# The MLP's second stage by seven half products, and pooling by adding DMAs, in a fused attention and mixer kernel

## The chip, the cores and the metric

The kernel runs on one core of one Trainium2 chip. The core has TensorE (PE, matrix products; PEld is its weight load), VectorE (DVE), ScalarE (ACT) and GpSimd (POOL). SyncE (SP), ACT and POOL issue DMAs. Each engine works through its own queue in order and waits on semaphores for the others. The metric is device time in microseconds (us), from the start to the end of one execution. A TensorE matmul takes a weight tile of 128 x 128 and streams up to 512 columns past it into one bank of PSUM, the accumulation memory; DVE or ACT drain the bank.

## What is computed

```
for each of 8 batches, 8 heads, 576 rows, head size 64:
    k_p, v_p = means of k, v over groups of 8 rows        # 72 rows
    attn     = softmax(q @ k_p.T / 8)
    x[:, head] = attn @ v_p                               # x: 576 x 512 a batch
u   = x + (relu(x.T @ w_tok1) @ w_tok2).T                 # mixes the 576 rows, hidden 256
out = u + relu(u @ w_ch1) @ w_ch2                         # mixes the 512 columns, hidden 1536
```

Inputs and output are float32; the products run on bfloat16 copies.

## The kernel before

**Units.** The last line above, the MLP, is most of the products. It is cut into nine units. Unit n below 8 has 512 rows of batch n, unit 8 has the 64 rows left over from each of the eight batches (`uT_tails`, `u_tails`). `unit_steps` (L439) is a unit. Its first stage makes twelve tiles of relu(u @ w_ch1), 128 hidden values by 512 rows, each by four matmuls of 512 columns (L451) and a relu on ACT into GT (L455). A half tile is two of these matmuls. The second stage makes four blocks of 128 rows by 512 columns, each by twelve matmuls with a piece of GT as weights and w_ch2 streaming (L474). DVE drains a block, adding u (L479), and SP stores it in two halves (L482). In unit 8 the last block is made in two halves of 256 columns (L463).

**What runs between.** `unit_steps` yields after every second matmul, 48 times a unit. At each yield `unit` (L515) runs the steps that a plan names for that place: FIRST, SECOND and THIRD for units 0 to 2, LATER for the rest (L489 to L501). The order on every engine's queue is exactly the order in which these steps are recorded. A step without a mark is for the next batch, `>` for the one after that, `<` for the unit's own. The steps:

- `lk3 lv3 lq3`: load k, v or q of the batch three ahead, by a DMA issued on POOL that also converts to bfloat16.
- `K0 K1 V0 V1`: pool half of the heads on POOL (`pool8`, L143): three additions, L146, L147 and L150 (k) or L152 (v). `k1`, `v1`: the same on DVE.
- `kpT`: turn the pooled k on PE (L195), copied by DVE (L197). `Q0 Q1`: turn q on DVE (L244).
- `s0` to `s3`: scores, eight small matmuls (L255) and two exponentials on ACT (L261).
- `av0` to `av4`: attention times v, eight small matmuls (L293), a reciprocal and a scaling on DVE (L305, L311), which give x.
- `at0 at1`: the row-mixing hidden layer (L339), relu on ACT for the first half and on DVE for the second.
- `u0` to `u4`: its second layer (L354) and the addition of x on DVE (L355). `u4` is the leftover rows, once for two batches.
- `t0` to `t4`: turn u on PE (L364) with a copy on DVE (L365). From batch 4 on instead: `M0 M2 M4 M` write u to memory and read it back in pieces on SP, and `T0` to `T4` turn the pieces on DVE (L387, L393). The first stage of the next unit needs these.

Before unit 0 a HEAD of steps makes batch 0. PSUM has eight banks: three for single tiles (`ps_one`), four as two pairs for scores and av (`ps_two`), one for turned tiles (`ps_tr`).

Of the kernel before, what the change touches and what calls it, by code (L numbers as in the profile page):

```python
# [13 lines left out]
PE = mybir.EngineType.PE  # L14
POOLE = mybir.EngineType.Pool
DVE = mybir.EngineType.DVE
ACT = mybir.EngineType.Activation
SYNC = mybir.EngineType.SP


@with_exitstack
def kernel(
# [30 lines left out]
    singles = ctx.enter_context(tc.tile_pool(name="singles", bufs=1))  # L53
    raw = ctx.enter_context(tc.tile_pool(name="raw", bufs=2))
# [34 lines left out]

    def load_kv(b, src, key):  # L90
        t = loaded[b, key] = raw.tile([SP, H, POOL, D], BF16, name=key + "r")
        if b == 0:
            for h0, h1, j0, j1 in ((0, HP, 0, BP), (0, H, BP, SP), (HP, H, 0, BP)):
                kv(t, src, b, h0, h1, j0, j1)
        else:
            kv(t, src, b, 0, H)
# [59 lines left out]
    def batch_steps(b):  # L156
# [29 lines left out]
        def pool(eng, t, g):  # L186
            def go():
                hs = slice(g * HP, (g + 1) * HP)
                pool8(eng, loaded[b, t], hs, st["kp"][:, g] if t == "k" else st["vp"][:, hs, 0:D], t == "k")
            return go  # L190

        def kpT():
            ps = ps_tr.tile([P, 4, SP], BF16, name="pt")
            for i in range(4):
                nc.tensor.transpose(out=ps[:, i, :], in_=st["kp"][:, i // 2, i % 2].rearrange("j l d -> j (l d)"),  # L195
                                    identity=ident[0:SP, 0:SP])
            nc.vector.tensor_copy(out=st["kD"].rearrange("p g e j -> p (g e j)"), in_=ps.rearrange("p i j -> p (i j)"))  # L197
# [82 lines left out]
        def av(c):  # L280
            def go():
# [4 lines left out]
                den = outp.tile([P, 2, 4], FP32, name="den")  # L286
# [19 lines left out]
                if first and c == 1:  # L306
                    for h in range(H):
                        nc.scalar.activation(out=dst[:, h * D:(h + 1) * D], in_=view[:, h // 4, h % 4, 0:D],
                                             func=AF.Copy, scale=den[:, h // 4, h % 4:h % 4 + 1])
                else:  # L310
                    nc.vector.tensor_tensor(out=dst.rearrange("p (a h d) -> p a h d", a=2, d=D),  # L311
                                            in0=view[:, :, :, 0:D],
                                            in1=den[rows, :, :, None].broadcast_to([n, 2, 4, D]), op=ALU.mult)
# [14 lines left out]
        def relu(m, ps):  # L328
            if m == 0:
# [28 lines left out]
        def uT(c):  # L358
            def go():
                src = st["u"][:, c, :] if c < 4 else u_tails[:, b // 2, :]  # L360
                dst, o = (late("uT"), c * P) if c < 4 else (uT_tails, b // 2 * P)
                ps = ps_tr.tile([P, 4, P], BF16, name="pt")
# [54 lines left out]
        for g in range(2):  # L417
            name[f"vpool{g}"] = ppool(g)
# [6 lines left out]
        for i in range(4):  # L425
            name[f"Q{i}"], name[f"s{i}"] = (lambda: None) if i % 2 else qD(i // 2), score4(i // 2, i % 2)
        for c in range(5):
            name[f"av{c}"], name[f"u{c}"], name[f"t{c}"] = av(c), u(c), uT(c)
            name[f"at_{c}"], name[f"T{c}"] = at_tile(c), blocks(c)
# [9 lines left out]
    def unit_steps(n, st):  # L439

        GT = gtp.tile([P, NM, 4 * P], BF16, name="GT")
        uT = uT_tails if n == B else st["uT"]
        if n < B and "paired" in st:
            pairs = uT.rearrange("f k n -> f (k n)").rearrange("f (k n e) -> f k n e", k=2, e=2)
            blocks = [pairs[:, kk // 2, :, kk % 2] for kk in range(4)]
        else:
            blocks = [uT[:, kk, :] for kk in range(4)]
        for m in range(NM):
            ps = ps_one.tile([P, 512], FP32, name="p1")
            for kk in range(4):  # L450
                nc.tensor.matmul(out=ps, lhsT=w_ch1[:, kk, m * P:(m + 1) * P], rhs=blocks[kk],  # L451
                                 start=(kk == 0), stop=(kk == 3))
                if kk == 1:
                    yield
            nc.scalar.activation(out=GT[:, m, :], in_=ps, func=AF.Relu)  # L455
            yield
        for c in range(4):
            if n == B and c == 3:
                for a in range(2):
                    cols = slice(a * 256, (a + 1) * 256)  # L460
                    ps = ps_one.tile([P, 512], FP32, name="p1")
                    for m in range(NM):
                        nc.tensor.matmul(out=ps[:, 0:256], lhsT=GT[:, m, c * P:(c + 1) * P], rhs=w_ch2[:, m, cols],  # L463
                                         start=(m == 0), stop=(m == NM - 1))
                    o_sb = outp.tile([P, DM], FP32, name="o")[:, 0:256]
                    nc.vector.tensor_tensor(out=o_sb, in0=ps[:, 0:256], in1=(u_tails if n == B else st["u"])[:, c, cols], op=ALU.add)
                    for half in range(2):
                        (nc.scalar if half else nc.sync).dma_start(
                            out=out[2 * c + half].rearrange("(p r) n -> p r n", r=BR)[:, 8, cols],
                            in_=o_sb[half * BP:(half + 1) * BP, :])  # L470
                continue
# [6 lines left out]
            o_sb = outp.tile([P, DM], FP32, name="o")  # L478
            nc.vector.tensor_tensor(out=o_sb, in0=ps, in1=(u_tails if n == B else st["u"])[:, c, :], op=ALU.add)  # L479
            for half in range(2):  # L480
                b, r = (2 * c + half, 8) if n == B else (n, 2 * c + half)
                nc.sync.dma_start(out=out[b].rearrange("(p r) n -> p r n", r=BR)[:, r, :],  # L482
                                  in_=o_sb[half * BP:(half + 1) * BP, :])
            yield


    HEAD = """c0 c1 d8 q0 d1 q1 d5 kp0 kp1 kt0 d2 o0 e0 kt1 kp2 kp3 o1 e1 kt2 kt3 q2 q3 d2 o2 e2 vpool0 o3 d1 vpool1 e3 d2
              av1 av0 av2 d2 av3 at_0 at_2 av4 at_1 at_3 d2 at_4 X0 X1 X2 A0 A1 A2 X3 A3 d3"""
    FIRST = {0: "<u0 K0 lv2 V0", 1: "<u1", 2: "<u2", 3: "<u3 k1", 7: "Q0 Q1 Q2", 9: "Q3", 14: "kpT v1",  # L489
             16: "s0", 18: "s1", 20: "s2 lk3 lq3 lv3", 22: "s3", 24: "av0", 26: "av1", 28: "av2", 30: "av3", 32: "av4",  # L490
             34: "at0 >K0 >K1", 35: "at1 >V0", 37: "u0", 38: "u1", 39: "u2", 40: "t0", 41: "u3", 42: "t1 u4", 44: "t2", 45: "t3",
             47: "t4"}
    SECOND = {0: "kpT Q0 Q1 >K0 >K1 lk3", 1: "Q2 Q3 v1 lq3 lv3 >V0 >V1", 4: "s0", 6: "s1", 9: "s2", 12: "s3", 14: "av0", 16: "av1",
              18: "av2", 20: "av3", 22: "av4", 24: "at0", 25: "at1", 27: "u0", 28: "u1", 29: "u2 t0", 31: "u3 t1", 33: "t2 >Q0",
              35: "t3 >Q1", 37: ">kpT >Q2 >Q3", 39: ">s0", 42: ">s1", 45: ">s2", 47: ">s3"}
    THIRD = {0: ">K0 >K1 >V0 >V1 lk3 lq3 lv3", 1: "av0", 3: "av1", 5: "av2", 7: "av3", 9: "av4", 11: "at0 >Q0", 12: "at1",
             14: "u0", 15: "u1", 17: "u2 t0", 18: "u3", 19: "t1 u4", 21: "t2 >Q1", 23: "t3", 25: "t4 >kpT", 26: ">Q2 >Q3",
             27: ">s0", 29: ">s1", 32: ">s2", 35: ">s3", 38: ">av0", 40: ">av1", 42: ">av2", 44: ">av3", 46: ">av4"}
    LATER = {0: ">K0 >K1 >V0 >V1 lk3 lq3 lv3 at0", 1: "at1", 3: "u4 M4", 4: "u0", 6: "u1 M0", 7: "u2", 9: "u3 M2 M",
             11: ">Q0", 12: ">Q1", 14: ">Q2", 16: ">Q3", 18: ">kpT", 22: ">s0", 24: "T0", 26: ">s1 T1", 28: "T2",  # L500
             30: ">s2 T3", 32: "T4", 34: ">s3", 37: ">av0", 39: ">av1", 41: ">av2", 43: ">av3", 45: ">av4"}  # L501
    warm = singles.tile([P, 512], BF16)

    def head(s):
        if s[0] == "d":
            ps = ps_tr.tile([P, 512], FP32, name="pt")
# [8 lines left out]
    def unit(n, at):  # L515
        if n + 2 < B:
            batches[n + 2][0]()
        for i, _ in enumerate(unit_steps(n, batches[n][2] if n < B else None)):
            for s in at.get(i, "").split():
                if s[0] == "l":  # L520
                    load(s[1], n + int(s[2]))
                    continue
# [5 lines left out]
    with tc.manual_schedule(engines={PE, POOLE, DVE, ACT, SYNC}):  # L528
# [59 lines left out]
```

## Time and profile before

| | us |
|---|---|
| time, median of 3 runs | 285.08 (284.79 to 285.76) |
| the profiled execution | 285.26 |
| its span, first to last instruction | 283.5 |
| start of unit 0's first matmul | 24.95 |
| start of unit 7's first stage | 237.71 |
| end of the last matmul | 279.71 |

Parts of the profile that are read below: the page's busy times; stretches of the span with each engine's busy time; the chain that ended last, in order of time; groups of instructions by line and shape (instructions' total and mean time, then the idle time before them and what ended it); the timeline; and DMA issues with size and median time from issue to landing. L numbers are lines of the kernel.

### The profile page before, as it was taken

Reading aid. Unit: us, or ns where it says so; the run is one execution under the profiler, and the core shown is the slowest. Engines: PE = TensorE matmul, PEld = TensorE weight load, DVE = VectorE, ACT = ScalarE, POOL = GpSimd, SP = SyncE. Lnnn points to the kernel's source line nnn. Section 1 sums busy time; section 2 is a strip of 40 time slices with the busy share of each in tenths; the row PEclk is TensorE's granted clock in tenths of the full one; section 3 lists DMA queues with packets and bytes.
Section 4 is the critical chain, followed back from the end, with each engine's and each line's share of the span. In section 5 each row is a group of like instructions: output and inputs, shape, how many; then the busy total and the mean of one; then the engine's idle time right before and its main releaser. Section 6 shows DMA issues by size and latency. Waiting matters only on the chain.

```text
span 283.5 us, 4515 instructions
## 1 busy us (share of the span) xinstructions
PE 274.8 (97%) x1816; PEld 130.3 (46%) x1816; DVE 138.2 (49%) x265; ACT 110.3 (39%) x193; POOL 140.1 (49%) x124
## 2 busy tenths in 40 slices
PE   8999899999999999999999999999999999999994
PEld 3755335444553544354445443544354444444443
DVE  5466977777583756175247434833383141011012
ACT  2543481029404642604751366046603512612600
POOL 8584894999999939974993796000000000000000
PEclk9999999999999999999999999999999999999999
DMA  7999999960893187159649955325132445015014
GB/s 148 194 202 207 204 205 200 234 135 2 123 166 74 39 118 132 43 96 202 143 90 151 222 139 81 82 58 129 39 76 56 126 78 112 3 37 111 2 39 110
DMA packets 36837, 32.68 MB, mean 115 GB/s; under 512 B 14288, under 2 KB 30288, under 8 KB 36816
## 3 DMA queue, kind: packets, MB, share of 16 engines
q0 software_dynamic: 18672, 17.64, 39.2%
q1 hardware_dynamic: 17984, 14.62, 21.9%
q8 instruction: 14, 0.23, 0.3%
q10 hardware_dynamic: 160, 0.13, 0.2%
q14 instruction: 7, 0.06, 0.1%
HBM read 38.21 MB, written 11.80 MB: 176 GB/s over the span
## 4 chain that ended last, share of the span: by engine, by line
PE 91%; DVE 5%; ACT 2%; issue 1%
PE p L451 31%; PE p L474 31%; PE p L354 6%; PE p L339 5%; PE p L255 4%; PE p L293 3%; PE pt L508 3%; ACT ex L261 2%; PE pt L364 1%; DVE t L146 1%; PE p L463 1%; PE p L273 1%; PE p L322 1%; DVE qD L244 1%; PE p L411 1%; PE p L226 1%
## 5 line engine op out<-in xcount | busy, mean ns | idle before, releaser
L474 PE MATMUL p<-w_ch,GT 128*128 128x512 bf16 x420 | 102.3, 379 | 0.0
L451 PE MATMUL p<-uT,w_ch 128*128 128x512 bf16 x384 | 96.6, 383 | 0.0
L455 ACT ACTIVATE GT<-p 128x512 bf16<-128x512 f32 x108 | 64.3, 596 | 82.4 <-PE p L451 82.4
L451 PEld LDWEIGHTS <-w_ch 128*128 128x128 bf16 x432 | 39.8, 97 | 48.9 <-issue 4.1
L474 PEld LDWEIGHTS <-GT 128*128 128x128 bf16 x420 | 37.6, 98 | 41.4 <-issue 3.7
L261 ACT ACTIVATE ex<-p 72x576 bf16<-72x576 f32 x56 | 33.1, 642 | 26.1 <-PE p L255 26.1
L479 DVE TENSOR_TENSOR o<-p,u 128x512 f32<-128x512 f32 x32 | 21.9, 684 | 36.6 <-PE p L474 36.6
L146 POOL TENSOR_TENSOR t<-kr 72x1024 f32<-72x1024 bf16 x13 | 27.9, 2143 | 23.6 <-DMA kr<-in_k_dram 23.0
L147 POOL TENSOR_TENSOR t<-t 72x512 f32<-72x512 f32 x25 | 33.5, 1339 | 2.0
L355 DVE TENSOR_TENSOR u<-p,x 128x512 bf16<-128x512 f32 x32 | 22.1, 690 | 14.0 <-PE p L354 13.9
L146 POOL TENSOR_TENSOR t<-vr 72x1024 f32<-72x1024 bf16 x12 | 25.5, 2122 | 1.1 <-DMA vr<-in_v_dram 0.4
L311 DVE TENSOR_TENSOR x<-p,den 128x512 bf16<-128x512 f32 x30 | 20.7, 691 | 1.0
L330 ACT ACTIVATE AT<-p 128x512 bf16<-128x512 f32 x8 | 4.8, 597 | 39.4 <-PE p L339 36.6
L293 PEld LDWEIGHTS <-ex 72*128 72x128 bf16 x320 | 15.4, 98 | 9.9 <-DVE x L311 0.8
L354 PE MATMUL p<-AT,w_tok 128*128 128x512 bf16 x64 | 19.0, 378 | 0.0
L387 DVE STREAM_TRANSPOSE uT<-v 128x256 uint32<-128x256 uint32 x16 | 6.1, 419 | 24.6 <-DMA v<-mem 24.6
L293 PE MATMUL p<-vp,ex 72*128 72x65 bf16 x320 | 16.8, 194 | 0.5 <-DVE x L311 0.3
L255 PE MATMUL p<-qD,kD 32*72 32x288 bf16 x224 | 14.4, 298 | 0.7 <-DVE kD L197 0.4
L339 PE MATMUL p<-x,w_tok 128*128 128x512 bf16 x56 | 14.4, 379 | 0.0
L305 DVE RECIPROCAL den<-p 128x8 f32<-128x8 f32 (+1 forms) x39 | 8.0, 204 | 11.5 <-PE p L293 10.9
L150 POOL TENSOR_TENSOR kp<-t 72x256 bf16<-72x256 f32 x13 | 12.1, 928 | 1.0
L332 DVE TENSOR_SCALAR AT<-p 128x512 bf16<-128x512 f32 x8 | 5.5, 691 | 13.9 <-PE p L339 13.1
(88 smaller groups left out, 209.5 us busy)
## 6 DMA issues: line engine op xcount, KB each, us to landing
out_dram<-o SPq DMA_DIRECT2D x70, 128.0 KB, 2.4
kr<-in_k_dram POOLq DMA_DIRECT2D x7, 576.0 KB, 8.3
qb<-in_q_dram POOLq DMA_DIRECT2D x7, 576.0 KB, 11.7
vr<-in_v_dram POOLq DMA_DIRECT2D x7, 576.0 KB, 14.8
w_ch<-in_moe_w_ch_dram POOLq DMA_DIRECT2D x6, 512.0 KB, 13.3
mem<-u SPq DMA_DIRECT2D x8, 256.0 KB, 3.0
v<-mem SPq DMA_DIRECT2D x8, 160.0 KB, 3.8
v<-mem SPq DMA_DIRECT2D x8, 128.0 KB, 3.3
```

The source lines that it names most:

```text
L146: eng.tensor_tensor(out=t4[:, 0:n], in0=t[:, hs, 0:4], in1=t[:, hs, 4:8], op=ALU.add)
L147: eng.tensor_tensor(out=t4[:, 0:n, 0:2], in0=t4[:, 0:n, 0:2], in1=t4[:, 0:n, 2:4], op=ALU.add)
L255: nc.tensor.matmul(out=pss[l // 2][0:SP, l % 2, 0:SH], lhsT=st["kD"][quad, g, db, :], rhs=st["qD"][quad, g, half * SH:(half + 1) * SH, db] ...
L261: nc.scalar.activation(out=exv[:, h:h + 2], in_=pss[a][0:SP, :, 0:SH], func=AF.Exp, scale=scale)
L293: nc.tensor.matmul(out=halves[h // 4][:, (h % 4) * (D + 1):(h % 4 + 1) * (D + 1)], lhsT=st["ex"][:, h * S + n0:h * S + n0 + P], rhs=st["vp ...
L339: nc.tensor.matmul(out=ps, lhsT=w_tok1[:, c if c < 4 else 4 + par, m * P:(m + 1) * P], rhs=st["x"][:, c, :] if c < 4 else st["xt"], start= ...
L354: nc.tensor.matmul(out=ps, lhsT=w, rhs=a, start=(i == 0), stop=(i == len(mms) - 1))
L355: nc.vector.tensor_tensor(out=dst, in0=ps, in1=x, op=ALU.add)
L451: nc.tensor.matmul(out=ps, lhsT=w_ch1[:, kk, m * P:(m + 1) * P], rhs=blocks[kk], start=(kk == 0), stop=(kk == 3))
L455: nc.scalar.activation(out=GT[:, m, :], in_=ps, func=AF.Relu)
L474: nc.tensor.matmul(out=ps, lhsT=GT[:, m, c * P:(c + 1) * P], rhs=w_ch2[:, m, :], start=(m == 0), stop=(m == NM - 1))
L479: nc.vector.tensor_tensor(out=o_sb, in0=ps, in1=(u_tails if n == B else st["u"])[:, c, :], op=ALU.add)
```

## The change

1. **Seven products for eight.** In units 1 to 8 the second stage is taken as a 2 x 2 block product: rows in two halves of 256, hidden values in two halves of 768, columns in two halves of 256. Eight block products become seven, with sums and differences of blocks of GT (eight DVE instructions a unit, `=1a` to `=4b`) and of w_ch2 (eight once, at the head of unit 1). Each product is twelve matmuls of 256 columns, so a unit has 84 of these. Some products add up in the same bank: the bank x is drained after the first, the fourth and the last product, z after the third and the sixth. A drain adds a kept partial result or u; there are eight drains of 512 elements a unit. The rows' result leaves by stores of twice the size, the upper half of the rows after the sixth product, the lower half at the end. In unit 8 the last two products are made block by block, and each quarter of the lower half is stored on its own.
2. **Adding DMAs.** For batches 4 to 7 a k or v load is four DMAs in float32. The first brings rows 0 and 1 of each group of 8, the others (`+k3a`, `+k3b`, `+k3c`) add rows 2 to 7 onto them, each after the one before. One addition on POOL is left of the pooling.
3. **Plans.** The four plans are rewritten, with 45 places in units 1 to 8; unit 8 gets its own (LAST). `at1`'s relu goes from DVE to ACT after batch 0.
4. **Memory.** `ps_tr` goes, `ps_one` has four banks. GT has a fixed place. Tiles that only the head uses share their place with the sums.

```
+    def add_rows(b, key):
+        i = parts_of[b, key]
+        parts_of[b, key] = i + 1
+        src = (k if key == "k" else v)[b].rearrange("h (j i) d -> j h (i d)", i=POOL)
+        nc.gpsimd.dma_start(out=pair_sums(b, key), in_=src[:, :, 2 * i * D:2 * (i + 1) * D],
+                            accum_op=ALU.add if i else ALU.bypass)
...
+                i0, i1 = pair[0], pair[1]
...
+                eng.tensor_tensor(out=dst, in0=i0, in1=i1, op=ALU.add)
...
-            if m == 0:
+            if m == 0 or not first:
                 nc.scalar.activation(out=late("AT")[:, m, :], in_=ps, func=AF.Relu)
...
+    def g_sums(s):
+        S4, f, sec = fast["S"], *sums("ab".index(s[1]))
+        if s[0] == "3":
+            sub(S4[:, 2, f], GT[:, f, lo], GT[:, f, hi])
+        elif s[0] == "1":
+            nc.vector.tensor_tensor(out=S4[:, 0, f], in0=GT[:, f, hi], in1=GT[:, sec, hi], op=ALU.add)
+        elif s[0] == "2":
+            sub(S4[:, 1, f], S4[:, 0, f], GT[:, f, lo])
+        else:
+            sub(S4[:, 3, f], GT[:, sec, lo], S4[:, 1, f])
+
+    def weight_sums(part):
+        f, s = sums(part)
+        sub(fast["T"][:, 0, f], w_ch2[:, f, hi], w_ch2[:, f, lo])
+        sub(fast["T"][:, 1, f], w_ch2[:, s, hi], fast["T"][:, 0, f])
+        sub(fast["T"][:, 2, f], w_ch2[:, s, hi], w_ch2[:, f, hi])
+        sub(fast["T"][:, 3, f], w_ch2[:, s, lo], fast["T"][:, 1, f])
...
+        def product(ps, a, w, start, after, split=False):
+            for i in range(2):
+                for m in range(NH):
+                    nc.tensor.matmul(out=ps[i] if split else ps[:, i], lhsT=a(m)[:, i * P:(i + 1) * P], rhs=w(m),
+                                     start=start and m == 0 and (i == 0 or split), stop=(m == NH - 1),
+                                     skip_group_check=True)
+                    if (i * NH + m) % 4 == 3 and (i, m) != (1, NH - 1):
+                        yield
...
+        x, y = bank(last), bank()
+        s1 = keep("s1")
+        yield from product(x, lambda m: GT[:, m, lo], lambda m: w_ch2[:, m, lo], True,
+                           plus(s1, x, u1[:, :, lo]), last)
+        yield from product(y, lambda m: GT[:, NH + m, lo], lambda m: w_ch2[:, NH + m, lo], True, plus(oa[:, :, lo], y, s1))
+        z = bank()
+        s5 = keep("s5")
+        yield from product(z, lambda m: SG[:, 0, m], lambda m: TW[:, 0, m], True, plus(s5, z, u2[:, :, hi]))
+        s2 = keep("s1")
+        yield from product(x, lambda m: SG[:, 1, m], lambda m: TW[:, 1, m], False,
+                           plus(s2, x, u1[:, :, hi]), last)
+        if not last:
+            w = bank()
+            s4 = keep("s4")
+            yield from product(w, lambda m: GT[:, NH + m, hi], lambda m: TW[:, 3, m], True, plus(s4, w, u2[:, :, lo]))
+        yield from product(z, lambda m: SG[:, 3, m], lambda m: w_ch2[:, NH + m, hi], False, plus(oa[:, :, hi], z, s2))
+        store(n, 0, oa)
+        if last:
+            yield from product(x, lambda m: SG[:, 2, m], lambda m: TW[:, 2, m], False,
+                               plus(ob[:, :, hi], x, s5, store_part(hi)), True)
+            yield from product(x, lambda m: GT[:, NH + m, hi], lambda m: TW[:, 3, m], False,
+                               plus(ob[:, :, lo], x, u2[:, :, lo], store_part(lo)), True)
+        else:
+            def finish(i):
+                plus(ob[:, :, hi], x, s5)(i)
+                plus(ob[:, :, lo], x, s4)(i)
+            yield from product(x, lambda m: SG[:, 2, m], lambda m: TW[:, 2, m], False, finish)
+            store(n, 1, ob)
...
-    LATER = {0: ">K0 >K1 >V0 >V1 lk3 lq3 lv3 at0", 1: "at1", 3: "u4 M4", 4: "u0", 6: "u1 M0", 7: "u2", 9: "u3 M2 M",
-             11: ">Q0", 12: ">Q1", 14: ">Q2", 16: ">Q3", 18: ">kpT", 22: ">s0", 24: "T0", 26: ">s1 T1", 28: "T2",
-             30: ">s2 T3", 32: "T4", 34: ">s3", 37: ">av0", 39: ">av1", 41: ">av2", 43: ">av3", 45: ">av4"}
+SECOND = {3: "lk3", 4: "Q0", 5: "kpT", 6: "v1", 7: "lv3", 9: "Q1", 11: "=3a s0", 14: "s1 =3b", 16: "s2", 18: "s3",
+          19: "=1a av0", 21: "av1", 22: "av3 >K0", 23: "+k3a", 24: "av4", 25: "av2 +v3a", 26: "=1b", 27: "=2a",
+          28: ">K1 +k3b =2b at0", 29: ">Q1 at1", 30: ">kpT", 31: ">V0", 32: "u0 u3 =4a", 33: ">s2 +v3b u1",
+          36: "=4b", 38: ">s3 t0", 40: ">Q0 t3 u2", 41: ">s1", 42: "t1", 43: "t2 +k3c", 44: "lq3 >s0 >V1 +v3c"}
+LATER = {0: ">Q1 lv3", 1: "lk3", 5: ">K1", 6: "=3a at0 at1", 7: "u4 M4", 8: ">K0 u3 u1 u0", 10: "u2", 11: ">kpT M0",
+         13: ">Q0 >s2", 14: "M2 +v3a", 17: "M >s1 =1a", 19: "=2a =4a", 21: ">s3", 23: "=3b", 26: ">s0 +k3a",
+         27: "=1b", 28: "=2b", 29: "lq3 >V0 >V1", 31: "=4b", 32: ">av1", 33: "+v3b >av0", 36: ">av2", 39: "T0 T2",
+         40: "T1 T3 +k3b", 44: ">av3 >av4 +v3c +k3c T4"}
```

In the first three products of a unit, the drains keep s1, write the left half of the upper rows, and keep s5. In unit 0 the second stage stays as it was.

## The prediction

> **What bounds the kernel now.** First the page's busy shares and the granted clock (10 tenths throughout), then busy time by stretch, then the chain that ended last, then groups with shapes kept apart.
>
> ```profile
> PE 274.8 (97%) x1816; PEld 130.3 (46%) x1816; DVE 138.2 (49%) x265; ACT 110.3 (39%) x193; POOL 140.1 (49%) x124
> ```
>
> TensorE (PE) is busy nearly always. Its busy time is modelled, so the stretches count more (length, PE busy, its weight loads, DVE, ACT, POOL, clock, DMA share, GB/s):
>
> ```profile
> 25.00:42.30 17.30, 15.66 (x94) 6.19 (x93) 14.38 (x13) 10.28 (x20) 13.71 (x10) 1.00 1.22 206
> 42.30:61.20 18.90, 18.36 (x138) 9.64 (x136) 13.09 (x27) 1.67 (x4) 14.30 (x12) 1.00 1.09 201
> 110.40:125.50 15.10, 14.53 (x130) 6.77 (x128) 7.63 (x17) 5.20 (x9) 14.40 (x13) 1.00 0.32 65
> 153.60:169.90 16.30, 16.30 (x84) 6.96 (x82) 6.94 (x14) 7.57 (x13) 11.67 (x8) 1.00 0.85 177
> 169.90:183.00 13.10, 13.10 (x114) 6.20 (x112) 8.07 (x18) 4.72 (x9) 5.05 (x5) 1.00 0.50 91
> ```
>
> From 25 us on PE stands idle about 3.0 us in all, 1.6 of it in unit 0. So a later unit costs what PE's instructions cost, and the chain gives their price (start, us, what):
>
> ```profile
> 227.35 10.36 PE p L474 x48
> 277.08 2.63 PE p L463 x24
> ```
>
> A matmul of 512 columns costs 10.36/48 = 215.8 ns, one of 256 columns 2.63/24 = 109.6 ns. The rows for what else is priced:
>
> ```profile
> L474 PEld LDWEIGHTS <-GT 128*128 128x128 bf16 x420 | 37.6, 98 | 41.4 <-issue 3.7
> L463 PEld LDWEIGHTS <-GT 128*128 128x128 bf16 x24 | 2.4, 98 | 0.5
> L479 DVE TENSOR_TENSOR o<-p,u 128x512 f32<-128x512 f32 x32 | 21.9, 684 | 36.6 <-PE p L474 36.6
> L466 DVE TENSOR_TENSOR o<-p,u_tails 128x256 f32<-128x256 f32 x2 | 0.8, 424 | 1.5 <-PE p L463 1.5
> L365 DVE COPY uT<-pt 128x512 bf16<-128x512 bf16 x12 | 5.0, 420 | 2.4 <-PE pt L364 2.4
> L238 DVE COPY qT<-p 128x640 bf16<-128x640 bf16 x4 | 1.9, 488 | 0.9 <-PE p L236 0.9
> ```
>
> **Part A, the products.** Units 1 to 7 replace 48 x 215.8 ns = 10.36 us by 84 x 109.6 ns = 9.21 us: 1.15 us less each. Unit 8 had 36 wide and 24 half matmuls (7.77 + 2.63 = 10.40 us): 1.19 less. Sum 7 x 1.15 + 1.19 = 9.24 us off the path. The cover is that each of 36 more weight loads per unit hides under the matmul before it: the L463 row has 98 ns loads beside a pitch of 109.6 ns. Without it they cost 36 x 98 ns = 3.5 us a unit.
>
> [...]
>
> **Part B, VectorE.** Each unit gains eight sums of 768 bf16 elements, four more drains of 512, and loses one relu from unit 1 on; eight weight sums stand once at the head of unit 1. No row has a bf16 sum from SBUF. Lower bound, the bf16 copies: (488 - 420)/128 = 0.53 ns an element, so 420 + 256 x 0.53 = 0.56 us. Upper bound, the f32 rows: (684 - 424)/256 = 1.02 ns, so 0.95 us. I take 0.56, because every operand is bf16 as in L365. Following DVE instructions start some 0.09 us before the last one's recorded end (46.15 then 46.74 for a 0.68 us one), so I count 0.48 for a sum and 0.60 for a drain.
> In the steady plan (units 3 to 5) DVE has 6.94 + 8.07 = 15.0 us of work in 29.4; it becomes 15.0 - 0.6 + 4 x 0.6 + 8 x 0.48 = 20.6 us in about 28.2. The tight place is the end of the second stage: the transposes T0 to T3 of the next unit stand behind two drains, two sums, three av scalings and more, some 9.4 us, and first-stage matmuls wait for T3. PE has 9.2 + 0.45 (scores) + 5 x 0.26 (av) = 11.0 us there, and DVE starts 1.5 us into it. So it meets PE: 0.1 us a unit, 0.3 in all. At 0.95 us a sum it is 1.2 later: 3.3 in all. The PSUM banks held across products cost nothing: the next unit's first stage takes the three free ones first and needs x's after 2.7 us, when its two drains (1.2) are done.
>
> **Part C, units 1 and 2, where POOL and DVE collide.** The row shows what two-input work from SBUF does on both engines at once:
>
> ```profile
> 28.97 2.11 POOL L146 TENSOR_TENSOR t<-kr 72x1024 f32<-72x1024 bf16 x1 [2.81 <-DMA kr<-in_k_dram]
> 29.29 2.87 DVE L146 TENSOR_TENSOR t<-kr 72x1024 f32<-72x1024 bf16 x1
> 31.16 2.13 POOL L147 TENSOR_TENSOR t<-t 72x512 f32<-72x512 f32 x1
> 49.28 1.26 POOL L147 TENSOR_TENSOR t<-t 72x512 f32<-72x512 f32 x1
> ```
>
> DVE ends 1.08 us after POOL's instruction ended, and POOL's next takes 2.13 instead of 1.26: they take turns. Batch 3 is still pooled by POOL, 4.46 us each for K0, K1, V0, V1 (157.38 to 161.84 is one).
> Count t from unit 1's first matmul. DVE: last drain and memsets to 0.7, weight sums to 4.9, qD to 5.6, kD 5.9; PE reaches s0 at 12 half tiles x 0.432 + 0.25 = 5.4: a wait of 0.5. POOL's second batch-4 load waits for v1's first read (7.1 to 7.9), so K0 runs from 8.0. There DVE's sums 3a, 3b, 1a take turns with K0's three instructions and end near 13.7 instead of 10.5; behind them stand the av scalings, which free the av banks, so PE's third av waits 1.6 and later steps 0.7. POOL: K0 13.2, two adding DMAs of 0.85 (L87 row: 0.80) 14.9, K1 with its own turns near 21; PE reaches kpT of batch 3 at about 22, no more wait. Then DMA, V0, three DMA issues, V1: 33.5 to 34, against PE's av4 in unit 2 at 34.3. Sum 0.5 + 2.3 + 0.4 = 3.2 us. Bounds: 0.5 without collisions; 7 with sums of 0.95 and late landings ahead of V1. I take 3.2, because those POOL instructions are in the plan beside these sums.
>
> **Part D, the adding DMAs.** Each k or v load becomes four DMAs of 288 KB, each waiting for the one before on the same tile; POOL's queue holds lq and the K and V sums behind those waits. On POOL two adds of three vanish (4.46 us to 0.93 a piece) and 24 issues of 0.8 us come, both off the path. Landings:
>
> ```profile
> kr<-in_k_dram POOLq DMA_DIRECT2D x7, 576.0 KB, 8.3
> qf<-in_q_dram SPq DMA_DIRECT2D x2, 288.0 KB, 3.1
> q0 software_dynamic: 18672, 17.64, 39.2%
> ```
>
> A landing is bounded by 3.1 (same bytes, plain) and 8.3 us (same packets, four times the bytes read). POOL goes round once a batch in 3 x (landing + 0.85) + 2 us: 13.9 to 29.5 against a unit of 28. I take about 6 us (22.5), between the ends, since k and v share the queue. The cover is one unit of lead; price 0, at the upper end 1.5 a batch.
>
> [...] No row here shows an adding DMA.
>
> **Part E, the end.**
>
> ```profile
> 279.73 0.42 DVE L466 TENSOR_TENSOR o<-p,u_tails 128x256 f32<-128x256 f32 x1 [0.88 <-PE p L463]
> out_dram<-o SPq DMA_DIRECT2D x70, 128.0 KB, 2.4
> ```
>
> After PE's last matmul 3.8 us pass. Now 1 MB instead of 0.5 leaves in the last 3 us: SP has six issues of about 0.5 us from 1.7 us before the last matmul, so the last goes at +1.1 to +1.6, not +0.5. At the 209 to 240 GB/s seen there the bytes take 4.4 us: +0.1 to +1.5. I take 0.9. Elsewhere the larger stores through two buffers cost nothing: a buffer is used again a unit later, and a store lands in 2.4 us.
>
> **Part F.** kpT of unit 0 moves three half tiles later but two u steps behind it: its 1.1 us wait shrinks by 0.4, and v1, now behind Q0 and u2 on DVE, makes av1 wait about 0.4: nothing. Of the 1.4 us idle later, the two 0.5 us waits of kpT go with their places: -0.8. Removed ps_tr and the move of AT's relu to ACT (4.7 to 7.6 us busy in 13 to 16) cost nothing; ACT's slack is the cover, and a late AT would hold u0 by the 0.6 us of a relu.
>
> **Sum.** -9.24 + 0.3 + 3.2 + 0 + 0.9 - 0.8 = -5.6 us. The profiled execution took 285.26 (span 283.5), 0.18 over the median 285.08. So 285.08 - 5.6 = 279.5.
>
> **Rivals.**
> 1. The collisions of C hardly cost: 0.5 instead of 3.2 there: 276.8, and 275.5 with all old idle gone. For it: POOL and DVE were both busy at 42 to 61 us with 0.5 us lost. Against it: there DVE had no two-input SBUF work.
> 2. VectorE becomes the bound, sums at 0.95: 8 x 0.39 = 3.1 before s0, 3.0 more in B: 285.6, no change. Against it: L365.
> 3. Slower: adding DMAs land late. [...] If landing is 10.6 us, the round takes 36.4, batches 6 and 7 lose 8.4 each, POOL's K, then kpT and PE wait: 296.3. It decides from 7.8 us on (round = unit) and passes the time before at 8.7. For it: DMA share is 0.85 and 0.50 already in a steady unit, and packets of this queue took 39.2% x 283.5 x 16/18672 = 95 ns; 3456 more a batch at that price are 20 us of all engines. Against it: that price is for packets of 2 KB and more, these read 512 B.
> 4. Weight loads show (A's cover gone): 279.5 + 28 = 307.
>
> **Chances.** Forecast 0.58 (own range 277 to 283), rival 1 0.19, rival 2 0.08, rival 3 0.13, rival 4 0.02. Faster by over 0.3% (0.9 us, about what a measurement of this kernel can tell): the first two, half of rival 2, a small part of rival 3: 0.82; within 0.04; slower 0.14. The range reaches 275.5 to 285.5, leaving out most of rivals 3 and 4.
>
> **What would show it.** A: 84 half matmuls in about 9.2 us in unit 7, which nothing interleaves. B: the mean of the sums, 0.5 to 0.6 or 0.9. C: PE idle in units 1 and 2, released by DVE x or POOL kp. D: landing of the 288 KB DMAs, and PE waiting for POOL kp in units 3 to 5. E: the span's rest after PE's last matmul, 4.7 instead of 3.8. The prediction falls if PE waits for POOL kp in every steady unit, or if half matmuls have a pitch above 123 ns (10.36/84).

## The result, and the profile after

| us | before | after |
|---|---|---|
| median of the runs side by side | 284.94 (284.34 to 285.76, 4 runs) | 282.28 (281.39 to 286.58, 4 runs) |
| the profiled execution, its span | 285.26, 283.5 | 282.9, 281.1 |
| unit 1 | 32.88 | 38.41 |
| unit 2 | 32.49 | 30.10 |
| unit 3, 4, 5 | 28.15, 29.45, 28.58 | 26.80, 29.09, 27.29 |
| unit 6, 7, 8 | 26.07, 21.23, 20.91 | 24.79, 20.04, 19.72 |
| from the last matmul to the end of the span | 3.81 | 5.62 |

The ratio is 0.9895 (95% interval 0.9848 to 0.9942): the change saves 1.0% of the time, where 279.5 us, 2.0% less, was forecast. Units are cut at the first first-stage matmul of each in the timeline (unit 8 ends at the last matmul), so a piece can differ by 0.2 us from the chain's. Some executions of a kernel take over 1.5% longer than its fastest; the ratios and their intervals leave those out, the medians and extremes do not.

Units 5 to 8 are 1.2 to 1.3 us shorter each, about what their matmuls save. Unit 1 is 5.5 us longer instead, and the end 1.8. So the question is unit 1. The page of the changed kernel, parts 1, 3, 5 and 6:

```profile
PE 262.8 (93%) x2068; PEld 156.4 (56%) x2092; DVE 191.3 (68%) x364; ACT 113.0 (40%) x200; POOL 118.9 (42%) x116
...
q0 software_dynamic: 32112, 22.40, 54.0%
...
L573 PEld LDWEIGHTS <-GT 128*128 128x128 bf16 x288 | 27.3, 98 | 6.4 <-issue 1.2
...
L551 DVE TENSOR_TENSOR area<-GT 128x768 bf16<-128x768 bf16 x16 | 13.6, 848 | 25.2 <-ACT GT L505 25.2
L126 POOL DMA_DIRECT2D kr<-in_k_dram x16 | 23.0, 1457 | 16.9 <-DMA kr<-in_k_dram 16.9
...
kr<-in_k_dram POOLq DMA_DIRECT2D x16, 288.0 KB, 7.1
vr<-in_v_dram POOLq DMA_DIRECT2D x16, 288.0 KB, 7.2
```

DVE went from 49% to 68%, and one of the sums (`=1a`, `=1b`, L551) has a mean of 848 ns. The same group in the stretch from 128 to 206 us, shapes kept apart, has another:

```profile
L551 DVE TENSOR_TENSOR area<-GT 128x768 bf16<-128x768 bf16 x6 | 3.3, 554 | 8.5 <-ACT GT L505 8.5
```

A mean over the span mixes fourteen sums of 0.55 us with two longer ones (4.60 and 1.20), and both lie in unit 1. The stretches (columns as before: length, PE, weight loads, DVE, ACT, POOL, clock, DMA share, GB/s) of unit 1, unit 4, unit 7 and the end:

```profile
59.24:97.65 38.41, 31.89 (x275) 17.71 (x278) 37.02 (x53) 16.12 (x28) 31.30 (x25) 0.96 0.60 93
155.00:184.00 29.00, 28.15 (x228) 16.75 (x230) 19.47 (x41) 12.33 (x22) 12.28 (x11) 1.00 1.11 184
235.72:255.76 20.04, 19.98 (x133) 12.88 (x132) 10.24 (x18) 7.17 (x12) 0.00 (x0) 1.00 0.20 54
275.50:281.10 5.60, 0.00 (x0) 0.00 (x0) 0.42 (x1) 0.00 (x0) 0.00 (x0) 0.74 0.62 163
```

In unit 1 DVE is busy 37.0 of 38.4 us and PE 31.9: there the bound has passed from PE to DVE. (The time that a started instruction stands counts as busy: one of the sums above is recorded with 4.60 us, where others of its shape take 0.55.) In unit 4 the DMA engines are full (share 1.11; before, 0.85 and 0.50 in that unit's two halves). Unit 7 is PE alone. What PE waited for, by the view of waits (total, times, longest; the fourth and fifth lie in the head and unit 0):

```profile
PE p L345 <- DVE x L363: 2.4, 2, 2.1
PE p L307 <- DVE qD L296: 2.2, 1, 2.2
PE p L247 <- DVE o L594: 1.7, 1, 1.7
PE p L648 <- DVE area L683: 1.2, 1, 1.2
PE p L247 <- POOL kp L193: 0.9, 1, 0.9
PE p L501 <- DVE uT L439: 0.8, 1, 0.8
```

Three of these are unit 1's: qD (q turned for the scores) at 70.20, x (a scaling of av) at 78.13, o (a drain, which frees the bank that kpT needs) at 86.39. The timeline shows what DVE did meanwhile:

```profile
66.67 2.79 DVE L195 TENSOR_TENSOR vp<-t 72x256 bf16<-72x256 f32 x1
67.04 2.13 POOL L189 TENSOR_TENSOR t<-kr 72x1024 f32<-72x1024 bf16 x1
...
69.38 0.77 DVE L296 STREAM_TRANSPOSE qD<-qb 128x576 uint32<-128x576 uint32 x1
70.08 2.17 DVE L544 TENSOR_TENSOR area<-GT 128x768 bf16<-128x768 bf16 x2
...
70.20 0.70 PE L307 MATMUL p<-qD,kD 32*72 32x288 bf16 x8 [2.16 <-DVE qD L296]
...
70.83 1.89 PE L501 MATMUL p<-uT,w_ch 128*128 128x512 bf16 x4
...
72.64 4.60 DVE L551 TENSOR_TENSOR area<-GT 128x768 bf16<-128x768 bf16 x1 [0.38 <-ACT GT L505]
...
72.65 2.01 POOL L126 DMA_DIRECT2D vr<-in_v_dram  x1
...
73.50 3.30 POOL L189 TENSOR_TENSOR t<-kr 72x1024 f32<-72x1024 bf16 x1
...
78.13 0.43 PE L345 MATMUL p<-vp,ex 72*128 72x65 bf16 x8 [2.06 <-DVE x L363]
```

The last addition of v1 (0.42 us alone) took 2.79: it ends 0.3 us after POOL's addition. The sum 1a (0.55 alone) took 4.60 and ends at 77.24, 0.44 after POOL's whole addition L189 at 76.80. Behind the first stands qD and so PE's scores, behind the second the scalings of av and so PE. After the 2.16 us wait four first-stage matmuls took 1.89 us, where four take 1.04 at 67.00; the granted clock was 0.50 from 70 to 73 us. Over DVE's rows of unit 1 the excess of these two, the two sums at 70.08 and four later sums beyond their undisturbed times is 2.4 + 4.0 + 1.1 + 0.7 + 1.6 + 1.5 = 11.3 us.

### The profile page after: what moved, and what is told of

Its sections match the earlier page's. It is cut to its first block, busy times and chain, and to the rows that moved or that the text cites. A ratio compares the mean times of both kernels' runs of the same rounds, so it can differ in the third digit from the quotient of the medians.

```text
span 281.1 us, 5168 instructions
## 1 busy us (share of the span) xinstructions
PE 262.8 (93%) x2068; PEld 156.4 (56%) x2092; DVE 191.3 (68%) x364; ACT 113.0 (40%) x200; POOL 118.9 (42%) x116
## 3 DMA queue, kind: packets, MB, share of 16 engines
q0 software_dynamic: 32112, 22.40, 54.0%
## 4 chain that ended last, share of the span: by engine, by line
PE 72%; DVE 14%; DMA 7%; issue 3%; ACT 1%; SPq 0%; POOL 0%; DVEq 0%; POOLq 0%
PE p L501 26%; PE p L573 21%; PE p L406 6%; PE p L391 5%; PE p L524 3%; DMA mem<-u 3%; PE p L307 3%; PE p L345 3%; DMA v<-mem 2%; DVE area L544 2%; DVE area L551 2%; DMA kr<-in_k_dram 2%; DVE t L189 1%; DVE x L363 1%; DVE u L407 1%
## 5 line engine op out<-in xcount | busy, mean ns | idle before, releaser
L573 PEld LDWEIGHTS <-area 128*128 128x128 bf16 x384 | 36.5, 98 | 5.9 <-issue 0.5
L573 PE MATMUL p<-area,area 128*128 128x256 bf16 x288 | 36.2, 273 | 0.0
L126 POOL DMA_DIRECT2D vr<-in_v_dram x16 | 22.2, 1426 | 25.6 <-DMA vr<-in_v_dram 19.6
L573 PEld LDWEIGHTS <-GT 128*128 128x128 bf16 x288 | 27.3, 98 | 6.4 <-issue 1.2
L407 DVE TENSOR_TENSOR u<-p,x 128x512 bf16<-128x512 f32 x32 | 21.0, 685 | 14.4 <-PE p L406 13.8
L551 DVE TENSOR_TENSOR area<-GT 128x768 bf16<-128x768 bf16 x16 | 13.6, 848 | 25.2 <-ACT GT L505 25.2
L126 POOL DMA_DIRECT2D kr<-in_k_dram x16 | 23.0, 1457 | 16.9 <-DMA kr<-in_k_dram 16.9
L594 DVE TENSOR_TENSOR s<-p,u 128x512 f32<-128x512 f32 x28 | 19.2, 687 | 11.7 <-PE p L573 11.7
L573 PE MATMUL p<-w_ch,GT 128*128 128x256 bf16 x192 | 23.8, 273 | 0.0
L594 DVE TENSOR_TENSOR o<-p,s 128x512 f32<-128x512 f32 (+1 forms) x32 | 20.4, 663 | 2.8 <-PE p L573 2.6
L345 PEld LDWEIGHTS <-ex 72*128 72x128 bf16 x320 | 14.4, 98 | 7.8 <-DVE x L363 3.8
L189 POOL TENSOR_TENSOR t<-kr 72x1024 f32<-72x1024 bf16 x5 | 11.8, 2355 | 7.1 <-DMA kr<-in_k_dram 7.0
```

The lines of the kernel that those rows point to most:

```text
L126: nc.gpsimd.dma_start(out=pair_sums(b, key), in_=src[:, :, 2 * i * D:2 * (i + 1) * D], accum_op=ALU.add if i else ALU.bypass)
L345: nc.tensor.matmul(out=halves[h // 4][:, (h % 4) * (D + 1):(h % 4 + 1) * (D + 1)], lhsT=st["ex"][:, h * S + n0:h * S + n0 + P], rhs=st["vp ...
L407: nc.vector.tensor_tensor(out=dst, in0=ps, in1=x, op=ALU.add)
L573: nc.tensor.matmul(out=ps[i] if split else ps[:, i], lhsT=a(m)[:, i * P:(i + 1) * P], rhs=w(m), start=start and m == 0 and (i == 0 or spli ...
L594: nc.vector.tensor_tensor(out=out[:, i], in0=ps[i] if type(ps) is list else ps[:, i], in1=other[:, i], op=ALU.add)
```

## The experiments

Three theories stood at the start. "Turns": DVE's two-input sums stand until POOL's two-input instruction is done, and unit 1's loss is that. "Amount": DVE has too much to do there, POOL or no POOL. "DMAs": the loss is the adding DMAs' contention. All code lines are against the changed kernel.

**POOL silent in unit 1.**

```
-22: "av3 >K0", ... 28: ">K1 +k3b =2b at0", ... 31: ">V0", ... 44: "lq3 >s0 >V1 +v3c"
+22: "av3", ... 28: "+k3b =2b at0", ... 44: "lq3 >s0 +v3c"
```

> Leaves out POOL's pooling of batch 3 (its K0, K1, V0 and V1 in unit 1; its keys and values are set to zero by small memsets), so the output of batch 3 is not the reference's. All VectorE work of unit 1 stays. Theory 'turns' (VectorE's bf16 sums wait until POOL's running two-input instruction has ended; 11.1 us of VectorE's 37.0 us busy time in unit 1 are such waits): the sums of unit 1 take 0.55 us each, unit 1 shrinks from 38.4 to 32.5-33.5 us, time 276.5-278. Rival 'amount' (VectorE simply has too much to do in unit 1, the eight weight sums of 4.4 us ahead of everything, and POOL does not matter): unit 1 stays at 37-38.5, time 281.5-282.5.

277.03 us median (274.76 to 278.54), ratio to before 0.9724 (0.9657 to 0.9792).

```profile
60.61:92.25 31.64, 30.36 (x275) 17.80 (x278) 27.22 (x55) 16.07 (x28) 14.91 (x14) 1.00 0.80 113
```

Unit 1 takes 31.64 us instead of 38.41, and all sixteen sums 0.49 to 0.56. DVE still does all its work: "amount" falls. POOL's presence costs at least 6.8 us there. Against 30.7 (31.86, the plain unit of the next run, less 1.15) a wait of 0.92 us for kD is left; the run's own memsets stand ahead of it, since its weight sums begin 1.43 us into the unit and the changed kernel's 0.62, so the price may be up to 7.7.

**Unit 1 plain.**

```
-        for i, _ in enumerate((unit_fast if n >= 1 else unit_plain)(n, st)):
+        for i, _ in enumerate((unit_fast if n >= 2 else unit_plain)(n, st)):
...
-        if n == 1:
+        if n == 2:
             fast["S"] = early.tile([P, 4, NM // 2, 256], BF16, name="area")
...
-11: "+k3a >Q0", 12: ">kpT av0", 16:
+11: "+k3a >Q0 W0", 12: ">kpT av0", 15: "W1", 16:        # W: weight_sums of one half
```

> Unit 1 keeps the eight products, with no sums; the weight sums move to unit 2 (half of them at step 11, half at step 15), units 2 to 8 as in the changed kernel. Both 'turns' and 'amount' take unit 1 back to about the 32.9 us that it had before (gain 5.5); PE pays 0.07 there already counted, unit 2 pays 0 to 1.5 us for 4.4 us of weight sums in its 30.5: time 277-278.5. If instead the loss sits in the adding DMAs that run beside unit 1 ('DMAs'), unit 1 stays above 36 and the time at 281-283.

276.53 us median (276.44 to 280.73), ratio 0.9709 (0.9682 to 0.9736). Unit 1 takes 31.86, unit 2 31.73 instead of 30.10, with one wait of 1.47 us behind the weight sums. So the half products of unit 1 bought 1.15 us of PE and cost 7.7 (38.41 against 30.71), and without them the change saves 2.9% instead of 1.0%.

**Batch 3 summed by DMAs too**, so that POOL has little to do in unit 1.

```
-SUMMED = 4
+SUMMED = 3
-37: "u3 u2 >K0 u4", ... 47: ">V0"}              SECOND = {3: "lk3", ... 7: "lv3"
+37: "u3 u2 >K0 u4 +k3a +v3a", ... 47: ">V0 +k3b +v3b"}   SECOND = {3: "lk3 +k2c", ... 7: "lv3 +v2c"
```

> Batch 3 too comes pair-summed by adding DMAs (three more for k and three more for v, put behind K0, V0 of batch 2 and at steps 3 and 7 of unit 1), so POOL's sums in unit 1 are four of 0.85 us instead of four of 4.46. 'Turns': unit 1 about 32-33 us, time 276-277.5. 'Amount': no change, 281.5-283. 'DMAs' (the adding DMAs and their contention are what costs): slower than 282.3, since six more of them meet unit 0's busiest stretch (203 GB/s): 283-288.

294.27 us median (292.94 to 296.2), ratio 1.0338 (1.0282 to 1.0394): slower, against the expectation of "turns" and beyond that of "DMAs". The waits, and one group:

```profile
POOL kr L126 <- DMA kr<-in_k_dram: 37.1, 12, 10.0
...
PE p L501 <- DVE uT L439: 8.6, 2, 4.7
```

```profile
L544 DVE TENSOR_TENSOR area<-w_ch,area 128x768 bf16<-128x768 bf16 x4 | 5.5, 1370 | 0.1
```

POOL's queue stood up to 10 us for the landing of one adding DMA, with batch 2's pooling behind it. That pooling slid into unit 1 and met the weight sums, now 1.4 us each instead of 0.55; unit 1 took 39.9. And units 3 and 4 took 31.6 and 33.6, because PE waited 4.65 and 3.98 us for uT: T0 to T3 stood for the read-back of u (v<-mem). The run does not test "turns", since it did not remove the meeting; it shows a second mechanism that the waits for POOL kp never showed.

**No half products, all else kept**: every unit plain, no sums.

```
-        for i, _ in enumerate((unit_fast if n >= 1 else unit_plain)(n, st)):
+        for i, _ in enumerate(unit_plain(n, st)):
```

> All units keep the eight plain products: no sums, no half products; adding DMAs, plans and stores stay as in the changed kernel. 'Turns': the adding DMAs cost next to nothing, so the time is that of before less the idle of kpT and the collisions in units 2 to 5, plus up to 1 us for the larger last stores: 283.5-285.5, units 1 to 3 at 32.5, 31.7 and 28 us. 'DMAs': the 6 us that the change did not deliver are theirs, 288-291.

286.94 us median (284.75 to 289.72, 10 runs), ratio 1.0036 (0.9993 to 1.0078); the profiled one 284.99. Adding DMAs and plans alone change nothing that can be told. Units 1 and 2 gain 1.0 and 1.2 us: the old waits of kpT, 0.7 and 0.5 us, are gone, and what gave the rest is not shown. Unit 4 loses 1.2 with a 0.73 us wait for uT, the end takes 5.5 instead of 3.8.

**No adding DMAs, half products kept.**

```
-SUMMED = 4
+SUMMED = 8
```

> The changed kernel, but batches 4 to 7 are loaded whole and pooled by POOL in three sums a piece as before (18 us of POOL a batch in units 2 to 5); no adding DMA is left. 'Turns': VectorE's eight sums of units 2 to 5 meet POOL's two-input instructions, their mean goes from 0.56 to 1.2-2.5 us there, and each of these units loses 1-4 us: 286-296. 'DMAs' (the adding DMAs are what the change lost by): faster than 282, 277-281. 'Amount': no change, 281.5-283.5.

288.41 us median (286.22 to 290.12), ratio 1.0106 (1.0036 to 1.0175). The sums between 101 and 163 us (units 2 and 3), by shape:

```profile
L544 DVE TENSOR_TENSOR area<-GT,area 128x768 bf16<-128x768 bf16 x4 | 6.3, 1567 | 0.0
L544 DVE TENSOR_TENSOR area<-GT 128x768 bf16<-128x768 bf16 x4 | 5.7, 1413 | 0.0
L544 DVE TENSOR_TENSOR area<-area,GT 128x768 bf16<-128x768 bf16 x4 | 5.5, 1366 | 0.1
```

With POOL adding in these units twelve of the sixteen sums take 1.4 to 1.6 us in the mean (the four of L551 0.79), and units 1, 2 and 3 are 4.4, 1.8 and 2.9 us longer than in the changed kernel. So the two parts pay only together: half products alone 288.4, adding DMAs alone 285 to 287, both 282.3, neither 284.9.

**The turn by itself**: with unit 1 plain, POOL gets four additions in unit 6 and four copies in unit 7, whose results go nowhere.

```
+        if n == 6: nc.gpsimd.tensor_tensor(out=o, in0=GT[0:SP, 0:2], in1=GT[0:SP, 2:4], op=ALU.add)
+        if n == 7: nc.gpsimd.tensor_copy(out=o, in_=GT[0:SP, 0:2])
-17: "M >s1 =1a"
+16: "p p p p", 17: "M >s1 =1a"
```

> Unit 1 plain with weight sums in unit 2 (276.5), and POOL, idle from unit 6 on, gets four instructions whose results go nowhere beside the sums 1a to 4b: in unit 6 four sums of 72x1024 bf16 to f32 (two inputs), in unit 7 four copies of the same size (one input). 'Turns': in unit 6 the VectorE sums beside them take 1.5-2.5 us instead of 0.55 and POOL's sums 2.1 to 3.3; if it is the two-input form that blocks, unit 7's stay at 0.55. The time: VectorE has 5 us of slack in unit 6 and 10 in unit 7, so 276.5-279. 'Amount': the sums stay at 0.55 in both, 276.5.

277.46 us (2 runs). Unit 6 took 24.89, unit 7 20.05, as without it (24.79 and 20.05).

```profile
211.71 8.76 POOL L667 TENSOR_TENSOR t<-GT 72x1024 f32<-72x1024 bf16 x4 [30.07 <-ACT GT L505]
...
218.80 2.09 DVE L551 TENSOR_TENSOR area<-GT 128x768 bf16<-128x768 bf16 x1 [3.17 <-ACT GT L505]
...
220.92 0.56 DVE L544 TENSOR_TENSOR area<-area,GT 128x768 bf16<-128x768 bf16 x1
```

POOL's four additions end at 220.47. The one sum that began in them, at 218.80, ends at 220.89: it stood until POOL had finished and ended 0.42 us later. POOL's additions kept their 2.19 us. The next sum takes 0.56. Of the copies only one met a sum (0.66 us), which decides nothing on copies. DVE had slack there (15.33 us busy of unit 6's 24.79 in the changed kernel), so the unit took no longer.

**Order in unit 1**: Q1 ahead of v1.

```
-5: "kpT", 6: "v1", 7: "lv3", 9: "Q1"
+5: "kpT Q1", 6: "v1", 7: "lv3"
```

> The changed kernel with one step of unit 1 moved: the transposition Q1 (for the scores s2, where PE stood 2.16 us) goes from step 9 to step 5, ahead of the pooling v1 that is blocked beside POOL. 'Order' (the three waits of unit 1 are single late instructions): 2.2 us less, unit 1 36.2, time about 280. 'Turns' as a throughput limit (VectorE is busy 37.0 of unit 1's 38.4 us, 11.1 of them held up by POOL, so whatever is moved, the sum remains): the wait at s2 goes and the later ones grow, unit 1 37.5-39, time 281.5-282.7.

The four runs took 282.55, 283.92, 288.3 and 539.6 us, so no gain can be told; the profile is of the second.

```profile
58.98:92.83 33.85, 30.53 (x275) 17.81 (x278) 32.37 (x53) 15.99 (x28) 26.99 (x20) 1.00 0.50 79
```

Both expectations on unit 1 were wrong: it fell to 33.85, by 4.6 us, more than the wait itself. DVE's busy time fell with it, from 37.0 to 32.4. Three sums (3a, 3b, 1a) that had taken 1.06, 1.19 and 4.60 us now took 0.54 each, though they lie inside an addition of POOL:

```profile
69.65 2.74 POOL L190 TENSOR_TENSOR t<-t 72x512 f32<-72x512 f32 x1
69.79 1.01 DVE L544 TENSOR_TENSOR area<-GT 128x768 bf16<-128x768 bf16 x2
70.73 0.54 DVE L551 TENSOR_TENSOR area<-GT 128x768 bf16<-128x768 bf16 x1
```

Here POOL's addition took 2.74 us instead of 1.47, so it was POOL that stood. And without the wait at s2 the granted clock stayed at 1.00. So unit 1 was not a fixed load. But the time did not fall. Units 2, 4 and 5 took 1.3, 2.1 and 1.6 us more, unit 4 with this wait:

```profile
183.09 3.21 PE L501 MATMUL p<-uT,w_ch 128*128 128x512 bf16 x7 [2.92 <-DVE uT L439]
```

**The end**: with unit 1 plain, half of unit 8's upper rows are stored early.

```
+        if last:
+            store(n, 0, oa, lo)      # after the second product
-        store(n, 0, oa)
+        store(n, 0, oa, hi if last else slice(0, 512))
```

> Unit 1 plain as in the run before with weight sums in unit 2 (276.5), and in unit 8 the lower columns of the first two row tiles are stored right after the second product (two DMAs of 128 KB some 9 us before the end) instead of with the upper ones (two of 256 KB). If the 1.8 us that the end became longer (5.6 after the last matmul instead of 3.8) come from 1 MB leaving in the last 3 us, 256 KB less brings 0.7-1.3 back: 275.2-275.9, rest after the last matmul 4.3-4.9. If the number of issues on the two queues sets it (last issue 2.1 us after the last drain), nothing: 276.4-276.8, or 0.3 more for two more issues.

The rest after the last matmul is 4.46 us instead of 5.60, as expected for the bytes. The whole time does not show it: 278.76 median (276.43 to 281.58), ratio 0.9772 (0.9696 to 0.9848). The same unit 0 took 32.8 to 36.2 us over these kernels, and unit 4's wait varied.

**The weight sums moved in unit 2** (steps 13 and 18; then 13 and 23), with the earlier store.

```
-11: "+k3a >Q0 W0", 12: ">kpT av0", 15: "W1", 16: ">V0 at0"
+11: "+k3a >Q0", 12: ">kpT av0", 13: "W0", 16: ">V0 at0", 18: "W1"      # the second kernel: 23: "W1"
```

> The run with the earlier store, and the two halves of the weight sums moved in unit 2 from steps 11 and 15 (ahead of the scalings that at0 waits for: PE stood 1.47 us there) to steps 13 and 18. 'Turns': that wait goes, 1.0-1.5 us off the run with the earlier store alone: about 274.3-275. 'Amount': VectorE is busy in unit 2 with 27 of 30 us either way, so another wait of the same size comes later and the time stays.

> Unit 1 plain, earlier store in unit 8, and the weight sums at steps 13 and 23 of unit 2: the second half now behind the transposition that s2 waits for (PE stood 1.09 us there with step 18). 'Turns': unit 2 falls from 31.2 to 30.3 us, so from unit 1's first matmul to the end 214.3 us instead of 215.3; the whole, with a first unit of 32.8 to 34, 272.5-275.5. 'Amount': another wait in unit 2 takes its place, 31 us, 274-276.5. Both beat the changed kernel's 282.3.

The first: 279.34 us median (275.22 to 281.43), ratio 0.9686 (0.9623 to 0.9748); unit 2 31.24, the old wait replaced by 1.09 us for qD, as "amount" had it. The second: unit 2 30.08 and no wait left in it, but 278.26 median (275.07 to 281.12), ratio 0.9699 (0.9663 to 0.9735). Its profiled execution, the longest of six, took 281.1, with unit 4 at 32.3 and the granted clock at 1.00 there. The timeline:

```profile
161.45 1.35 POOL L147 DMA_DIRECT2D qb<-in_q_dram  x1
...
165.74 6.13 SPq L432 DMA_DIRECT2D v<-mem  x4
...
179.92 1.42 DVE L439 STREAM_TRANSPOSE uT<-v 128x256 uint32<-128x256 uint32 x4 [4.66 <-DMA v<-mem]
```

and the same place in the run with unit 1 plain (unit 4 in 28.6):

```profile
154.81 1.94 POOL L147 DMA_DIRECT2D qb<-in_q_dram  x1
...
169.17 1.97 SPq L432 DMA_DIRECT2D v<-mem  x4
...
175.77 1.42 DVE L439 STREAM_TRANSPOSE uT<-v 128x256 uint32<-128x256 uint32 x4 [0.92 <-DMA v<-mem]
```

In the slower one q's load of 576 KB leaves 4.3 us ahead of the read-back, in the other 14.4 us, and such a load lands in 12 us (median 12.8 in the slower one, 12.0 in the other). The four read-backs then took 6.1 us to issue and 10.9 to land, against 2.0 and 4.8. Two executions prove little, but the others agree: PE waited over 0.8 us for uT six times in all profiled executions (1.19 to 4.65 us), each time with a q load still on its way when the first read-back left. Three times such a load cost less: 0, 0.65 and 0.73 us.

**Two adding steps instead of four**: the DMAs read packets of 1 KB, POOL adds twice.

```
-in_=src[:, :, 2 * i * D:2 * (i + 1) * D]
+in_=src[:, :, 4 * i * D:4 * (i + 1) * D]
+eng.tensor_tensor(out=two, in0=four[:, :, 0:2], in1=four[:, :, 2:4], op=ALU.add)
```

> As the run before it with the earlier store and the weight sums at steps 13 and 23, but batches 4 to 7 come by two DMAs a tensor (one plain, one adding) that read 1 KB packets, instead of four that read 512 B; POOL adds 4 to 1 in two sums a piece (some 2.1 us) instead of one (0.85). 'Contention' (in units 3 and 4 the adding DMAs keep the DMA engines busy the whole time, share 1.01 to 1.07, and POOL's queue, which waits for each landing, runs late, so that the q load meets the spill through DRAM that the transposes T0 to T3 wait for; PE stood 0.3 to 4.0 us there, differing from run to run): the share falls to 0.7-0.9, the waits for uT go below 0.3, unit 4 takes 28.1-28.4 each time, runs agree within 1.5 us; POOL's longer sums cost 0-1 us a unit: 272.5-275.5. Rival 'bytes' (the same bytes cost the same): waits of 0.3-4 us remain, 275-281, and POOL's sums come on top.

284.29 us median (280.54 to 285.18, 12 runs), ratio 0.9920 (0.9884 to 0.9956). Both expectations failed. The profile is of the longest run:

```profile
90.39:126.35 35.96, 31.99 (x288) 19.86 (x290) 32.94 (x56) 12.87 (x22) 25.16 (x24) 0.95 1.01 169
```

Packets of that queue fell from 32112 to 20336, but unit 2's DMA share is still 1.01, and POOL's extra additions met the sums: unit 2 took 36.0 instead of 30.1. Unit 3 had a wait of 3.99 us for uT. It is "turns" again, and it says little on the packets.

**No late q**: the queries of batches 6 and 7 are not loaded.

```
+        elif b >= 6:
+            nc.vector.memset(quarters(qb), 0.0)
```

> As the run with the weight sums at steps 13 and 23 (four adding DMAs a tensor), but the queries of batches 6 and 7 are not loaded (two DMAs of 576 KB in units 3 and 4 left out; their tiles are set to zero), so the output of these batches is not the reference's. 'q in front' (the q load, issued late by POOL's queue, lies ahead of the reads v<-mem that T0 to T3 wait for): the waits for uT ahead of units 4 and 5 fall under 0.4, unit 4 takes 28.1-28.5 in every run, the undisturbed runs come within 1 us of 273-275. Rival 'all of it' (the adding DMAs alone fill the engines): waits of 0.3 to 4 us remain in some runs, which spread over 274-281 as before.

274.99 us median (273.86 to 276.14), ratio 0.9649 (0.9607 to 0.9691). No wait for uT of 0.25 us or more is left, and unit 4 takes 28.6. The five runs lie within 2.3 us, not within 1; with the loads the six lay within 6. So q's loads are what the read-back met. Whether it is their place ahead of it or just their 576 KB was not tried apart.

## Why the prediction came out as it did

The direction and the range held; the likeliest time was 2.8 us too low, and 2.7 us were saved where 5.6 were forecast. That the time still fell into the forecast's own range, 277 to 283, is partly luck: C, D and E came out 4.5, 0.8 and 0.9 us worse than summed, and A, B and F 0.3, 0.3 and 1.4 better, with 0.7 from the start and unit 0, which were not in the sum. Step by step:

- **What bounds the kernel**: PE in units 2 to 8, as said. In unit 1 it is DVE, which the forecast never took as a bound (rival 2 had DVE as one, through slow sums everywhere).
- **A, the products**: right. The chain's piece of unit 7 is this; 9.17/84 = 109.2 ns (109.6 forecast).

```profile
246.76 9.17 PE p L573 x84
```

Units 7 and 8 are 1.19 us shorter each. The weight loads of 98 ns hide: 84 of them are 8.2 us, and the 84 matmuls still take 9.17 in all.
- **B, DVE's sums**: the lower bound, 0.55, was right wherever a sum met none of POOL's additions. The 0.3 us at the end of the second stage did not come: units 3, 5 and 6 are 1.35, 1.29 and 1.28 shorter.
- **C, the collisions**: the mechanism was right (the sums stand beside POOL's additions: 1a took 4.60 us, and all sixteen 0.49 to 0.56 with POOL silent), the size was not. 3.2 was taken; it is 6.8 to 7.7 in unit 1, up to above the upper bound of 7, and nothing in unit 2. Of the 7.7, 6.2 are PE standing longer and 1.5 its instructions taking longer (31.89 us busy against 30.41), with the clock at half from 70 to 73 us. The step that failed is "DVE's sums 3a, 3b, 1a take turns with K0's three instructions and end near 13.7": 1a ended 18.0 us into the unit (77.24 - 59.24). The forecast gave the three sums 3.2 us of standing together; 1a alone lost 4.05, through two DMA issues and a whole addition. The wait of the third av came, with 2.06 us for 1.6. But the forecast had a wait at s0 (0.5) where there was none, and passed over qD, which stood behind v1's blocked addition at s2 (2.16), kpT's wait for its bank (1.65) and the granted clock of 0.50 from 70 to 73 us, after the wait at s2.
- **D, the adding DMAs**: 7.1 to 7.2 us to land where 6 was taken, 1.44 us to issue where 0.85 was. By its own formula the round is 3 x (7.1 + 1.44) + 2 = 27.6 us against units of 26.8 to 29.1: the cover is used up, just. POOL kp was never late in units 3 to 5, as said. The step that failed is "price 0": it asked only who waits for these DMAs, not whose transfers they and POOL's late queue hit. That is u's way through memory to the next unit. In unit 4 the last write took 8.96 us and the last read-back 6.28 (before, no write there took over 5.39 and no read-back over 4.09), and q's load was on its way from 161.23 to 173.05, through most of the write. PE waited 0.8 us here, up to 4.65 in other kernels of this study.
- **E, the end**: +1.8 instead of +0.9. The last issue came 2.1 us after the last drain because one issue on each queue (275.64 on ACT, 275.68 on SP) took 1.4 us instead of 0.5 to 0.6. In the run with 256 KB stored earlier the last stores have as many issues, none takes over 0.7, and the rest after the last matmul is 4.46: so it is the bytes, as said.
- **F**: the plans brought 1.0 in unit 1 and 1.2 in unit 2 (the run without half products), not 0.8 in all; the waits of kpT account for 1.2 of these 2.2.

- **The rivals**: the collisions cost far more than the 0.5 us of rival 1, undisturbed sums take 0.55 and not 0.95 (2), no weight load shows (4). Rival 3 (adding DMAs late, deciding from a landing of 7.8 us) came near: its 10.6 us was an assumption and the landings were 7.1 and 7.2 in the median, but with issues of 1.44 its own formula decides from 7.2. What lagged then hit u's way through memory and not the pooled k.

Together: -9.5 (A, 8 x 1.19) + 7.7 (C, 38.41 against 30.71) + 0.8 (D) + 1.8 (E) - 2.2 (F) - 0.7 (start and unit 0) = -2.1, where the span shows -2.4.

In the experiment on the turn by itself the 2.09 us sum began in POOL's additions and ended 0.42 us after them, which fits a sum that stands until POOL is done. A wait for the one instruction that is running does not explain 1a: it lost 4.05 us (4.60 - 0.55), and the longest of POOL's instructions there has 3.30. When 1a began, POOL was issuing DMAs and no addition ran.

The best kernels here keep unit 1 plain: 0.9709 (0.9682 to 0.9736), and with the earlier store and moved weight sums 0.9699 (0.9663 to 0.9735), not told apart.

## What to carry to other kernels

Before a faster form puts two-input SBUF work on VectorE, look for the stages in which GpSimd does the same, and leave those stages as they are: one unit of nine took back over 70% of what the products gained (at least 6.8 us of 9.5). Where a queue of DMAs waits on its own landings, count the issue into the round (1.44 us beside a landing of 7.1 here), and ask which other transfers run late or are hit when it lags, not only who waits for its data. Judge single edits by the unit that they touch: a gain of 1 us in the time was hidden here by a start and a wait that vary by 3.

## What the runs showed of the hardware

- A two-input DVE sum can stand longer than one POOL instruction. 1a (0.55 us of work) began at 72.64, while POOL issued two adding DMAs (71.78 to 74.66), and ended at 77.24, 0.44 us after the addition behind them. In the run without adding DMAs a sum that began at 91.50, beside two plain issues, ended at 95.13, 0.43 us after the addition that followed (92.58 to 94.70); PE, which waited 1.97 us for it, went on at 95.19. A sum beside an issue with no addition close behind took 0.55 (142.57 in the changed kernel). What holds the sum through the issues is not shown.
- It can also go the other way: with Q1 ahead of v1, three sums one after the other took 0.54 us each, and POOL's addition beside them 2.74 instead of 1.47.
- An adding DMA issued by POOL with no other issue before it took 1.38 to 1.44 us (71.78, 79.21, 93.61), the plain first one of the same 288 KB 0.81 and 0.84 (66.21, 59.46). In the kernel without any sums on DVE adding ones took 1.38 to 1.41 (unit 4).
- The granted clock was 0.50 from 70 to 73 us (0.98 in the us before, 0.82 in the one after). PE had stood from 68.04 to 70.20.
